# Flipping P and x in 64-row halves, with one PSUM tile of two banks for both

## The chip, the cores and the metric

One core of a Trainium2 chip runs the program. The metric is the device time of one execution in microseconds (us). Engines are named as the profile names them: PE (TensorE matmul), PEld (its weight loads), DVE (VectorE), ACT (ScalarE), POOL (GpSimd), SP (SyncE, which issues DMAs).

## The reference

Attention over 8 batches, 8 heads, 576 tokens of 64 elements, with a causal window of 128 and a linear bias by head, and then a soft mixture of 8 experts with 4 slots each, on all 4608 tokens of 512 elements. Shapes and eps aside it is

```python
scores = q @ k.T / 8 ; scores = where(0 <= rel < 128, scores - slope * abs(rel), -1e9)
attn = softmax(scores) @ v                     # per batch and head
x = attn.transpose(0, 2, 1, 3).reshape(4608, 512)
logits = x @ phi                               # 4608 x 32 slots
d = softmax(logits, axis=0); slot_input = d.T @ x
h = relu(slot_input[e] @ w1[e]); slot_out = h @ w2[e]      # per expert e
out = softmax(logits, axis=1) @ slot_out
```

## The kernel before

A group is (b, t, g): batch b, a tile t of 128 tokens (t = 4 is the tail of 64), and half g of the heads, four heads to a group; the tail takes all eight. There are 72 groups. Scores and softmax have tokens on the partitions, so that row sums are free. The product with V needs P with keys on the partitions, and the logits and the dispatch sums need x both ways. So PE turns 128x128 pieces over by a matmul with the identity as moving operand: `flip` does it for the four pieces of P of a group (from `p4`, L351), `x_flip` for the four pieces of a token tile of x (L408). Each writes one PSUM bank: P goes to tile `pt`, x to tile `xq`. ACT copies them out, P in `split` (L358, to `pa`; on POOL two affine selects then part it into the strips before and on the diagonal), x in `x_keep` (L417, to `xn`).

PSUM has 8 banks of 512 fp32 elements per partition. Before, four banks are the tags xp, mi, pt, xq of `ps_1`, one tile each, and two score tiles `s4` have two banks each. At the end of the loop some flips go `to=` a bank that is free.

All engines run in the order that the code writes (`tc.manual_schedule`). Iteration i of the loop issues: `softmax_front` of group i on DVE (merge of the two key strips, row maximum, bias `nb`, inverse, and `normalise`, L306, of group i-1); `flip` and `split` of group i-3; copies due now ("act"); `values` of group i-4 (L387, P times V); the scores of group i+1 (L247/L254, for t = 0 L235/L240); `expo` (L341: four exponentials on ACT, which wait for `nb`, L292); and what is due late ("pe": `x_flip`, `logits`, `slot_flip` L465, `token_flip`, `slot_sum`, `slot_tail` L516; "dve": `token_max` L451, `slot_add` L522). `slot_sum` multiplies the dispatch weights of a batch with its x into `ap`, and `slot_add` adds that to `acc` with a rescaling, as an online softmax does. Odd batches b < 7 take the tail of two batches along: `slot_tail` adds it, and there alone `x_keep` stands in the "pe" list, which on ACT is behind the exponentials:

```python
            if tail:
                do("pe", i + 2, x_flip, b, 4)
                do("pe", i + 4, x_keep, b, 4)
                do("pe", i + 5, slot_tail, b)
                do("dve", i + 5, slot_add, b)
```

After the loop (here called the end of the attention) the last four groups ga, gb, gc, gd run by a list of their own: `flip(gb)`, `values(gb, ..., bank("xq"))`, `lane_rows`, `slot_sum(last)`, `join` (L601, adds up the lanes), `join_keep` (ACT, L604), `last_sum` (L651, copied by DVE, L654), `slot_inputs` (L660, which needs POOL's `comb`, L606). Then come the experts (`hidden` L931, `expert_out` L967) and the final combination (L991, L993).

Of the kernel before, what the change touches and what calls it, by code (L numbers as in the profile page):

```python
# [10 lines left out]
F32 = mybir.dt.float32  # L11
# [10 lines left out]
DM = H * D  # L22
E, SPE, F = 8, 4, 1024
NS = E * SPE
P = 128
# [43 lines left out]
def tile_attn_softmoe(  # L69
# [88 lines left out]
    front = ctx.enter_context(ExitStack())  # L158
    ps_s = front.enter_context(tc.tile_pool(name="ps_s", bufs=1, space=PSUM))
    s4s = [ps_s.tile([P, 4, 2 * P], F32, name=f"s4_{i}") for i in range(2)]  # L160
    free = [s4[:, 2 * h:2 * h + 2].rearrange("p u w -> p (u w)") for s4 in s4s for h in range(2)]
# [64 lines left out]
    def scores(i):  # L226
# [3 lines left out]
        if i == 0:  # L230
            parts = [ps_1.tile([P, 2, 2 * P], F32, tag=tag, name="s4_0") for tag in ("pt", "xp")]
        qt = qs[i % 3].rearrange("p (j w) -> p j w", w=width(t))
# [113 lines left out]
    def flip(key, us=ALL, to=None):  # L346
        s = st[key]
        if "pt" not in s or to is not None:
            s["pt"] = ps_1.tile([P, 4, P], F32, tag="pt", name="pt") if to is None else to
        for u in range(4)[us]:  # L350
            nc.tensor.transpose(s["pt"][:, u], s["p4"][:, u], ident)  # L351

    def split(key, us=ALL):
        s, t = st[key], key[1]
        i = number[key] % 2 if number[key] < n - 1 else 2
        m = len(range(4)[us])
        pa, pp = pas[i], pps[i % 2]
        nc.scalar.copy(pa[:, us], s["pt"][:, us])  # L358
        if 0 < t < 4:
            nc.gpsimd.affine_select(  # L360
                pp[:, us], pa[:, us], [[0, m], [-1, P]], ALU.is_gt, 0.0, base=0, channel_multiplier=1)
            nc.gpsimd.affine_select(  # L362
                pa[:, us], pa[:, us], [[0, m], [1, P]], ALU.is_ge, 0.0, base=0, channel_multiplier=-1)
        elif t == 4:
            nc.gpsimd.affine_select(
                pp[:, us], pa[:, us], [[0, m], [0, 2], [-1, TAIL]], ALU.is_gt, 0.0, base=0, channel_multiplier=1)
            nc.gpsimd.affine_select(
                pa[0:TAIL, us], pa[0:TAIL, us], [[0, m], [0, 2], [1, TAIL]], ALU.is_ge, 0.0,
                base=0, channel_multiplier=-1)
        s.update(pd=pa, pp=pp)  # L370
# [34 lines left out]
    def x_flip(b, t, to=None):  # L405
        xq = ps_1.tile([P, DM], F32, tag="xq", name="xq") if to is None else to
        for j in range(NPAIR):
            nc.tensor.transpose(xq[:, P * j:P * j + P], x_of(b, t)[:, j], ident)  # L408
        st["xq", b, t] = xq
# [6 lines left out]
    def x_keep(b, t, copy=nc.scalar.copy):  # L416
        copy(xn_of(b, t), st.pop(("xq", b, t)))  # L417

# [86 lines left out]
    def slot_sum(b):  # L505
        dn = st["d", b]
        ap = ps_1.tile([P, DM], F32, tag="mi" if b < last else "pt", name="ap")
        for c in range(lanes(b)):
            nc.tensor.matmul(
                ap[NS * c:NS * c + NS], lhsT=dn[:, NS * c:NS * c + NS], rhs=xns[c],  # L510
                start=True, stop=(c < 3 or not with_tail(b)),
            )
        st["a", b] = ap
# [85 lines left out]
    def join():  # L599
        st["join"] = ps_1.tile([P, 512], F32, tag="pt", name="join")  # L600
        nc.tensor.matmul(st["join"][fin], lhsT=comb, rhs=acc, start=True, stop=True)  # L601
# [45 lines left out]
    def last_sum(h):  # L647
        ap = ps_1.tile([P, DM // 2], F32, tag=("xq", "xp")[h], name="ap")
        cols = slice(DM // 2 * h, DM // 2 * (h + 1))
        for c in range(3):  # L650
            nc.tensor.matmul(  # L651
                ap[NS * c:NS * c + NS], lhsT=st["dnf"][:, NS * c:NS * c + NS],
                rhs=xn_of(last, FINAL[c])[:, cols], start=True, stop=True)
        (nc.scalar.copy if h else nc.vector.tensor_copy)(sums[0:3 * NS, cols], ap[0:3 * NS])  # L654
# [122 lines left out]
    with tc.manual_schedule(engines=ORDERED):  # L777
# [34 lines left out]
        def bank(tag):  # L812
            return ps_1.tile([P, NPAIR, P], F32, tag=tag, name="bank")

# [4 lines left out]
        token_copy(last)  # L819
        flip(gb)  # L820
        split(gb, LO)
# [15 lines left out]
        values(gb, range(0, 2), bank("xq"))  # L837
        flip(gd, LO)
        split(gd, LO)
# [30 lines left out]
        load_weight()  # L870
        x_flip(last, 4)
        x_flip(last, 0, free[1])
# [34 lines left out]
    front.close()  # L907
    ps_o = ctx.enter_context(tc.tile_pool(name="ps_o", bufs=4, space=PSUM))

    def load_weights(k):  # L910
# [11 lines left out]
    def hidden(nb, kk):  # L922
        if kk == 0:
            hp[nb] = ps_1.tile([P, 512], F32, tag=("xp", "pt")[nb], name="hp")
        for g in range(2):
# [20 lines left out]
    def hidden_flip(nb):  # L946
        hq = ps_1.tile([P, 512], F32, tag="xq", name="hq")
        for i in range(4):
# [9 lines left out]
    def expert_out(m, f, g):  # L958
        w = MW[m]
        if m not in ops:  # L960
            ops[m] = ps_1.tile([P, w], F32, tag=("xp", "pt")[m % 2], name="op")
        fu = UW // w
# [17 lines left out]
    def slot_stack(j):  # L980
        ot = ps_1.tile([P, P], F32, tag=("xq", "mi")[j % 2], name="ot")
        for i in range(2):
# [139 lines left out]
```

## Time and profile before

| | |
|---|---|
| median of 3 runs | 296.63 us (296.41 to 296.80) |
| span of the profiled execution | 294.4 us; the median of the runs is 2.2 us longer (no time of its own is given for this execution) |
| PE busy | 94% of the span |
| DVE busy | 82% |
| ACT busy | 71% |
| POOL busy | 32% |
| flips of P, PE (L351) | 282 matmuls, 45.9 us |
| flips of x, PE (L408) | 136 matmuls in tile xq, 22.1 us |

Busy times of PE overlap between successive matmuls, so the time a group of them takes is read from the distance of their starts. In rows of the timeline the columns are the start in us from the span's start, the duration of the group, engine, line, operation, output and inputs, shapes, the number of instructions, and in brackets the idle time before with what ended it. The body of the loop lies between about 17 and 217 us.

### The profile page before, as it was taken

The page shows a single profiled execution, that of the slowest core. Times are in us where ns is not written, and L with a number is a line of the kernel's source. Part 1 is how long each engine was busy: PE and PEld are TensorE (multiplying, and loading weights), DVE is VectorE, ACT ScalarE, POOL GpSimd, SP SyncE. Part 2 cuts the span into 40 slices and gives each one's busy share as a digit, 9 for nine tenths or more (in the row PEclk, how much of TensorE's full clock was granted, in tenths as well). Part 3 has the DMA queues.
Part 4 walks back from the last instruction along what each step waited for, and adds up shares of the span by engine and source line. Part 5 has one row for each costly group of instructions (what it writes and reads, how often), then busy time and mean ns, then how long its engine had stood idle before and what let it go on. Part 6 is the DMA issues. An engine that isn't in the chain of part 4 may idle for free. (4 is left out here: it accounts for less than half of the span.)

```text
span 294.4 us, 13061 instructions
## 1 busy us (share of the span) xinstructions
PE 275.9 (94%) x5131; PEld 195.7 (66%) x5131; DVE 240.3 (82%) x745; ACT 208.2 (71%) x814; POOL 93.0 (32%) x207
## 2 busy tenths in 40 slices
PE   8598999999999999999999999999999999999980
PEld 4366777777677777776776777667766743587650
DVE  3889999999989999998999999979996454655450
ACT  2778898987988988987898978978886421044450
POOL 2033525542444354244415442445452011000000
PEclk9689999999999999999999999999999999999997
DMA  6635368878676887868588967776456599998997
GB/s 192 217 112 144 110 194 251 277 218 288 203 265 209 268 284 235 260 213 273 180 281 262 292 217 248 248 222 222 141 164 234 160 314 355 411 400 327 345 365 264
DMA packets 36754, 72.59 MB, mean 247 GB/s; under 512 B 4402, under 2 KB 15316, under 8 KB 36692
## 3 DMA queue, kind: packets, MB, share of 16 engines
q1 hardware_dynamic: 35972, 71.24, 72.8%
q8 instruction: 41, 0.67, 0.9%
q10 hardware_dynamic: 720, 0.51, 0.6%
q14 instruction: 21, 0.17, 0.2%
HBM read 62.29 MB, written 9.44 MB: 244 GB/s over the span
## 5 line engine op out<-in xcount | busy, mean ns | idle before, releaser
L341 ACT ACTIVATE area<-s,nb 128x128 f32<-128x128 f32 x288 | 102.3, 375 | 19.8 <-DVE nb L292 17.5
L306 DVE TENSOR_SCALAR area<-area,rs 128x128 f32<-128x128 f32 x286 | 79.5, 339 | 0.7 <-DVE nb L292 0.3
L387 PE MATMUL xp<-area 128*64 128x128 f32 (+1 forms) x1104 | 75.4, 272 | 1.1 <-POOL rs L297 0.4
L387 PEld LDWEIGHTS xp<-area 128*64 128x64 f32 x1104 | 56.5, 137 | 15.9 <-issue 9.3
L341 ACT ACTIVATION_READ_ACCUMULATOR area<-s,nb 128x1 f32 x288 | 61.3, 213 | 0.0
L289 DVE TENSOR_REDUCE s<-s 128x4 f32<-128x512 f32 x71 | 49.5, 698 | 2.2
L358 ACT COPY area<-pt 128x512 f32<-128x512 f32 (+1 forms) x72 | 42.3, 590 | 11.6 <-PE pt L351 11.3
L351 PE MATMUL pt<-unit_r,area 128*128 128x128 f32 x282 | 45.9, 285 | 2.7 <-ACT area L306 2.2
L297 POOL TENSOR_SCALAR rs<-sm 128x4 f32<-128x4 f32 x70 | 13.8, 197 | 99.0 <-ACT area L341 98.2
L351 PEld LDWEIGHTS pt<-unit_r,area 128*128 128x128 f32 x282 | 32.0, 143 | 17.2 <-PE s L254 5.0
L254 PE MATMUL s<-kq 64*32 64x160 f32 x1792 | 42.4, 303 | 0.1
L360 POOL TENSOR_SCALAR_AFFINE_SELECT area<-area 128x512 f32<-128x512 f32 x48 | 31.4, 655 | 26.7 <-ACT area L358 25.6
L269 DVE COPY_PREDICATED s<-cst,s 128x512 f32<-128x512 int32 x48 | 32.9, 686 | 1.3 <-PE s L254 1.3
L362 POOL TENSOR_SCALAR_AFFINE_SELECT area<-area 128x512 f32<-128x512 f32 x48 | 31.5, 657 | 3.3
L254 PEld LDWEIGHTS s<-kq 64*32 64x32 f32 x1792 | 29.9, 108 | 1.0 <-issue 0.4
L408 PE MATMUL xq<-unit_r,area 128*128 128x128 f32 x136 | 22.1, 285 | 0.8 <-ACT area L417 0.7
L403 ACT COPY area<-xp 128x512 f32<-128x512 f32 (+1 forms) x37 | 20.7, 559 | 2.9 <-PE xp L387 2.3
L247 PE MATMUL s<-ramp,ones 64*32 64x320 bf16 x448 | 18.9, 313 | 2.7 <-ACT area L341 2.2
L417 ACT COPY area<-xq 128x512 f32<-128x512 f32 x34 | 20.7, 608 | 0.2 <-PE xq L408 0.2
L408 PEld LDWEIGHTS xq<-unit_r,area 128*128 128x128 f32 x136 | 14.5, 141 | 7.4 <-issue 4.1
L993 ACT COPY ob<-po 128x512 f32<-128x512 f32 x19 | 10.4, 591 | 11.4 <-PE po L991 10.7
L993 DVE COPY ob<-po 128x512 f32<-128x512 f32 x17 | 11.2, 687 | 6.6 <-PE po L991 5.8
(169 smaller groups left out, 328.4 us busy)
## 6 DMA issues: line engine op xcount, KB each, us to landing
w<-w SPq DMA_DIRECT2D x53, 512.0 KB, 5.2
out<-ob SPq DMA_DIRECT2D x36, 256.0 KB, 3.9
kq<-q_t SPq DMA_DIRECT2D x69, 128.0 KB, 3.2
kq<-k_t SPq DMA_DIRECT2D x32, 256.0 KB, 3.8
area<-v_n SPq DMA_DIRECT2D x31, 256.0 KB, 4.2
area<-w SPq DMA_DIRECT2D x8, 512.0 KB, 4.8
area<-v_n SPq DMA_DIRECT2D x12, 128.0 KB, 3.1
kq<-w SPq DMA_DIRECT2D x3, 512.0 KB, 6.3
```

Source lines behind the costliest of these rows:

```text
L254: nc.tensor.matmul(s4[32 * c:32 * c + 32, 2 * par + jj, 32 * r:32 * r + WIN], lhsT=qt[rows, 2 * h + jj if t == 4 else jj, 32 * r:32 * r + 32],
L269: nc.vector.copy_predicated(s4[:, :, P:2 * P], bc(mask_u, 1, 4), s4[:, :, 0:P])
L289: nc.vector.tensor_reduce(st[key]["mx"][:, us], merged(key, us), axis=AX.X, op=ALU.max, negate=True)
L306: mul(p4[:, u], p4[:, u], st[key]["rs"][:, u:u + 1])
L341: nc.scalar.activation(s["p4"][:, u], merged(key, u), AF.Exp, bias=s["nb"][:, u:u + 1], scale=SCALE, accum_out=s["sm"][:, u:u + 1],)
L351: nc.tensor.transpose(s["pt"][:, u], s["p4"][:, u], ident)
L358: nc.scalar.copy(pa[:, us], s["pt"][:, us])
L360: nc.gpsimd.affine_select(pp[:, us], pa[:, us], [[0, m], [-1, P]], ALU.is_gt, 0.0, base=0, channel_multiplier=1)
L362: nc.gpsimd.affine_select(pa[:, us], pa[:, us], [[0, m], [1, P]], ALU.is_ge, 0.0, base=0, channel_multiplier=-1)
L387: nc.tensor.matmul(xp[D * par:D * par + D, j, 0:w], lhsT=v_slot[b, t - 1 + ph][0:rows, D * h:D * h + D], rhs=src[:, 2 * par + i] if t < 4 ...
L408: nc.tensor.transpose(xq[:, P * j:P * j + P], x_of(b, t)[:, j], ident)
L993: copy_by[by](ob, po)
```

## The change

One tile `pq` of two banks takes the place of the tags pt and xq. The columns 0 to 255 of both banks belong to P, 256 to 511 to x. A piece is no longer one transpose of 128 rows but two of 64 rows, which stand on the upper and the lower half of PE's rows; row half r writes bank r. `split` and `x_keep` read their halves from both banks. 69 of the 72 flips of P and 33 of x are made so. The flips with `to=` at the end of the attention stay whole, and use single banks of `pq` (or of `s4`); the tiles for `join`, `last_sum(0)`, the last `slot_sum` and others of the end, which had been tiles of the tags pt and xq, are now parts of `pq` too. The experts' tiles get a pool of their own (`ps_2`) after `pq` is freed. Waits are set by the tile: what writes any part of `pq` waits for the copies that still read it.

```diff
+    pq = ps_s.tile([P, 2, 4 * P], F32, name="pq")
+    pq_p, pq_x = pq[:, :, 0:2 * P], pq[:, :, 2 * P:4 * P]
...
     def flip(key, us=ALL, to=None):
         s = st[key]
-        if "pt" not in s or to is not None:
-            s["pt"] = ps_1.tile([P, 4, P], F32, tag="pt", name="pt") if to is None else to
+        if to is not None:
+            s["pt"] = to.rearrange("p u (r w) -> p u r w", r=2)
+            for u in range(4)[us]:
+                nc.tensor.transpose(to[:, u], s["p4"][:, u], ident)
+            return
+        s["pt"] = pq_p.rearrange("p r (u w) -> p u r w", u=4)
         for u in range(4)[us]:
-            nc.tensor.transpose(s["pt"][:, u], s["p4"][:, u], ident)
+            for r, rows in enumerate(half):
+                nc.tensor.transpose(s["pt"][:, u, r], s["p4"][rows, u], ident[rows, rows])
...
-        nc.scalar.copy(pa[:, us], s["pt"][:, us])
+        nc.scalar.copy(pa[:, us].rearrange("p u (r w) -> p u r w", r=2), s["pt"][:, us])
...
     def x_flip(b, t, to=None):
-        xq = ps_1.tile([P, DM], F32, tag="xq", name="xq") if to is None else to
+        x = x_of(b, t)
+        if to is not None:
+            for j in range(NPAIR):
+                nc.tensor.transpose(to[:, P * j:P * j + P], x[:, j], ident)
+            st["xq", b, t] = to.rearrange("p (j r w) -> p j r w", j=NPAIR, r=2)
+            return
+        xq = pq_x.rearrange("p r (j w) -> p j r w", j=NPAIR)
         for j in range(NPAIR):
-            nc.tensor.transpose(xq[:, P * j:P * j + P], x_of(b, t)[:, j], ident)
+            for r, rows in enumerate(half):
+                nc.tensor.transpose(xq[:, j, r], x[rows, j], ident[rows, rows])
         st["xq", b, t] = xq
...
-        copy(xn_of(b, t), st.pop(("xq", b, t)))
+        copy(xn_of(b, t).rearrange("p (j r w) -> p j r w", j=NPAIR, r=2), st.pop(("xq", b, t)))
...
-        ap = ps_1.tile([P, DM], F32, tag="mi" if b < last else "pt", name="ap")
+        ap = ps_1.tile([P, DM], F32, tag="mi", name="ap") if b < last else pq[:, 0]
...
-        st["join"] = ps_1.tile([P, 512], F32, tag="pt", name="join")
+        st["join"] = pq[:, 0]
...
-        ap = ps_1.tile([P, DM // 2], F32, tag=("xq", "xp")[h], name="ap")
+        ap = ps_1.tile([P, DM // 2], F32, tag="xp", name="ap") if h else pq[:, 1, 0:DM // 2]
...
-            return ps_1.tile([P, NPAIR, P], F32, tag=tag, name="bank")
+            return pq[:, ("pt", "xq").index(tag)].rearrange("p (u w) -> p u w", u=4)
...
-        flip(gb)
+        flip(gb, to=bank("pt"))
...
-        flip(gd, LO)
+        flip(gd, LO, bank("pt"))
...
-        x_flip(last, 4)
+        x_flip(last, 4, pq[:, 1])
```

No instruction changes its place on an engine; the flips become longer lists, and waits change. Line numbers of the changed kernel are larger by 3 to 18: `flip` is L359 in halves and L354 whole, `x_flip` L423 and L417, `split` L366, `x_keep` L432, `slot_tail` L531, `slot_add` L537.

The first place is on PE, at the tail of an odd batch. Before, between the last of `slot_sum` and `slot_tail`:

```order
L509 MATMUL ap<-area,dn 32x512 x3
L351 MATMUL pt<-unit_r,area 128x128 [waits PE_49]
L351 MATMUL pt<-unit_r,area 128x128 x3
L387 MATMUL xp<-area 64x128 [waits Activation_49,Pool_49]
L387 MATMUL xp<-area 64x128
```

and now:

```order
L524 MATMUL ap<-area,dn 32x512 x3
L359 MATMUL pq<-unit_r,area 128x64 [waits Activation_49]
L359 MATMUL pq<-unit_r,area 128x64 x7
L395 MATMUL xp<-area 64x128 [waits PE_49,Pool_49]
L395 MATMUL xp<-area 64x128
```

The flip of P has 8 matmuls of half the width, and waits for ACT's count now. The copy that it waits for is the x_keep of the tail tile, which on ACT stands here, in the changed kernel, behind the four exponentials and ahead of this flip's own copy:

```order
L344 ACTIVATE area,sm<-s_1_84,nb 128x128 [waits DVE_49,Pool_49]
L344 ACTIVATE area,sm<-s_1_84,nb 128x128 x3
L432 COPY area<-pq 128x512 [waits PE_49]
L366 COPY area<-pq 128x512 [waits PE_49,Activation_49,Pool_49]
L552 ACTIVATE ln<-ln 128x160
```

Before, the same two copies stood in the same order there, out of two tiles (xq and pt). A little further on the same PE list follow the scores of t = 0 (L243, 64 rows and 128 columns), the flip of x and `slot_tail`; now:

```order
L243 MATMUL s_1_84<-kq 128x128 [waits DMAHW4_49]
L243 MATMUL s_1_84<-kq 128x128 x3
L423 MATMUL pq<-unit_r,area 128x64 [waits Activation_49]
L423 MATMUL pq<-unit_r,area 128x64 x7
L531 MATMUL ap<-area,dn 32x512
```

Here the order is as it was; the flip of x has the array shape of the scores ahead of it.

The second place is on PE at the end of the attention, around `flip(gb)`. Before:

```order
L426 MATMUL lp<-area,phi 32x128 [waits DVE_49]
L426 MATMUL lp<-area,phi 32x128 x7
L351 MATMUL pt<-unit_r,area 128x128 [waits PE_49]
L351 MATMUL pt<-unit_r,area 128x128 x3
L465 MATMUL dp<-unit_r,lg 128x64 [waits Activation_49]
```

and now:

```order
L441 MATMUL lp<-area,phi 32x128 [waits DVE_49]
L441 MATMUL lp<-area,phi 32x128 x7
L354 MATMUL pq<-unit_r,area 128x128 [waits Activation_49]
L354 MATMUL pq<-unit_r,area 128x128 x3
L480 MATMUL dp<-unit_r,lg 128x64 [waits Activation_49]
```

The flip is whole in both; its wait for PE's own count has become one for ACT, the copy of the x tile flipped just before.

The third place is on DVE, where the last `slot_add` stands. Before:

```order
L596 TENSOR_SCALAR comb<-cst,rows 128x32 [waits PE_49]
L597 TENSOR_TENSOR lg<-lg,rows 1x128 [waits Activation_49]
L522 SCALAR_TENSOR_TENSOR acc<-acc,al,ap 64x512 [waits PE_49]
L633 COPY dn<-dp 128x96 [waits DVE_49,PE_49]
L580 TENSOR_REDUCE lg<-lg 1x32 [waits DVE_49]
L654 COPY area<-ap 96x256 [waits PE_49]
```

and now:

```order
L611 TENSOR_SCALAR comb<-cst,rows 128x32 [waits PE_49]
L612 TENSOR_TENSOR lg<-lg,rows 1x128 [waits Activation_49]
L537 SCALAR_TENSOR_TENSOR acc<-acc,al,pq 64x512 [waits Activation_49]
L648 COPY dn<-dp 128x96 [waits DVE_49,PE_49]
L595 TENSOR_REDUCE lg<-lg 1x32 [waits DVE_49]
L669 COPY area<-pq 96x256 [waits PE_49,Activation_49]
```

`slot_add` and the copy of `last_sum` now wait for ACT's copies as well.

More of the change, by code (lines that the diff above doesn't have):

```diff
@@ L230, in scores @@
         if i == 0:
-            parts = [ps_1.tile([P, 2, 2 * P], F32, tag=tag, name="s4_0") for tag in ("pt", "xp")]
+            parts = [ps_1.tile([P, 2, 2 * P], F32, tag="xp", name="s4_0"), pq[:, 0].rearrange("p (u w) -> p u w", u=2)]
+            parts = parts[::-1]
         qt = qs[i % 3].rearrange("p (j w) -> p j w", w=width(t))
@@ L908, in tile_attn_softmoe @@
     ps_o = ctx.enter_context(tc.tile_pool(name="ps_o", bufs=4, space=PSUM))
+    ps_2 = ctx.enter_context(tc.tile_pool(name="ps_2", bufs=1, space=PSUM))
+    bank_of = {"xp": ps_1, "mi": ps_1, "pt": ps_2, "xq": ps_2}
     def load_weights(k):
@@ L923, in hidden @@
         if kk == 0:
-            hp[nb] = ps_1.tile([P, 512], F32, tag=("xp", "pt")[nb], name="hp")
+            tag = ("xp", "pt")[nb]
+            hp[nb] = bank_of[tag].tile([P, 512], F32, tag=tag, name="hp")
         for g in range(2):
@@ L946, in hidden_flip @@
     def hidden_flip(nb):
-        hq = ps_1.tile([P, 512], F32, tag="xq", name="hq")
+        hq = ps_2.tile([P, 512], F32, tag="xq", name="hq")
         for i in range(4):
@@ L960, in expert_out @@
         if m not in ops:
-            ops[m] = ps_1.tile([P, w], F32, tag=("xp", "pt")[m % 2], name="op")
+            tag = ("xp", "pt")[m % 2]
+            ops[m] = bank_of[tag].tile([P, w], F32, tag=tag, name="op")
         fu = UW // w
@@ L980, in slot_stack @@
     def slot_stack(j):
-        ot = ps_1.tile([P, P], F32, tag=("xq", "mi")[j % 2], name="ot")
+        tag = ("xq", "mi")[j % 2]
+        ot = bank_of[tag].tile([P, P], F32, tag=tag, name="ot")
         for i in range(2):
```

## The prediction

> **What bounds the kernel now.** I read the page's busy table first, then a table of busy time over a window, and then DVE's waits.
>
> ```profile
> PE 275.9 (94%) x5131; PEld 195.7 (66%) x5131; DVE 240.3 (82%) x745; ACT 208.2 (71%) x814; POOL 93.0 (32%) x207
> ```
>
> PE looks like the bound, with 94% of the 294.4 us span. But the span holds stages with different limits: the attention loop to about 217 us, its end to 239, and then the experts. So I take a window inside the attention loop: two periods of two batches, 63.38 to 172.94. Columns: length; busy time of PE, PEld, DVE, ACT, POOL; granted clock, DMA share, GB/s.
>
> ```profile
> 63.38:172.94 109.56, 108.48 (x2192) 79.73 (x2185) 104.22 (x333) 94.58 (x390) 44.13 (x97) 1.00 0.77 247
> ```
>
> PE is 1.1 us short of full and DVE 5.3. Which of the two sets the pace is told by who waits. DVE's waits on others from 60 to 215 us (columns: total, times, longest) are these two alone:
>
> ```profile
> DVE acc L522 <- PE ap L516: 4.1, 3, 1.5
> DVE fine L451 <- ACT lg L446: 1.6, 3, 0.5
> ```
>
> Six waits, 5.7 us in 155. Between them DVE runs without a stop, so a faster PE gains nothing there: a microsecond off PE counts only where it shortens one of these six. PE is late for DVE at two places per odd batch: slot_tail (L516), whose sum slot_add (L522) takes, and the token copy (L446) behind PE's logits.
>
> **What a flip costs, and in halves.** These rows show a flip of four pieces in the loop, then weight loads by shape (mean ns after the busy time), then three small transposes.
>
> ```profile
> 86.24 0.66 PE L408 MATMUL xq<-unit_r,area 128*128 128x128 f32 x4
> 86.73 0.60 PE L351 MATMUL pt<-unit_r,area 128*128 128x128 f32 x4
> 87.26 0.99 PE L387 MATMUL xp<-area 128*64 128x128 f32 x14
> ```
> ```profile
> L351 PEld LDWEIGHTS pt<-unit_r,area 128*128 128x128 f32 x282 | 32.0, 143 | 17.2 <-PE s L254 5.0 <-ACT area L341 4.8 <-issue 2.9
> L240 PEld LDWEIGHTS s<-kq 64*128 64x128 f32 x128 | 9.4, 207 | 0.2
> L983 PEld LDWEIGHTS ot<-so,ostk 128*128 128x128 f32 x8 | 1.4, 188 | 0.6 <-DVE so L977 0.2 <-DVE so L978 0.2
> L676 PEld LDWEIGHTS dp<-unit_r,lg 32*128 32x128 f32 x3 | 0.3, 136 | 0.9 <-issue 0.9
> ```
> ```profile
> 245.70 0.26 PEld L676 LDWEIGHTS dp<-unit_r,lg 32*128 32x128 f32 x3 [0.86 <-issue]
> ```
>
> A flip takes 86.73−86.24 = 0.49 to 87.26−86.73 = 0.53 us of PE's time, about 0.12 a piece. Fewer rows do not shorten a load of 128 columns (136 ns with 32 rows, 143 with 128). But small loads can follow faster: three span 0.26 us, (0.26−0.136)/2 = 62 ns apart. And loads into the two row halves of the array (L240) take 207 ns each beside 188 for a lone one (L983), so a pair seems to cost little more than one. In halves a piece is two loads of 64 rows and two streams of 64 columns. Bounds: nothing saved (a pair costs what one piece did) and 0.19 us a flip (a pair at about 75 ns against 0.12). I take 0.12 us a flip, a piece at some 90 ns: the loads remain and only the streams are halved. 102 flips (69 of P, 33 of x) in halves make some 12 us of PE work, of which DVE's pace hides all but what reaches the six waits.
>
> By the Trainium skill ("TensorE: Matmul & The Clock Gate", LDWEIGHTS) a load takes its columns divided by 1.2, 107 ns for 128 columns, whatever the rows. Loads 62 ns apart at L676 disagree with it as a pace. By it a flip would stay at some 0.43 us and save at most 0.1, which is rival 2.
>
> **The new waits.** P and x now share two banks in one tile, so each flip of P must let ACT's copy of x (x_keep) end, and each flip of x ACT's copy of P (split). At most places the copy ends before PE gets there, mostly by 0.3 us or more. Not so at the tail of an odd batch, b = 1, 3, 5:
>
> ```profile
> 79.13 0.16 DVE L292 TENSOR_SCALAR nb<-s 128x4 f32<-128x4 f32 x1
> 80.13 0.66 PE L351 MATMUL pt<-unit_r,area 128*128 128x128 f32 x4
> 80.42 0.37 ACT L341 ACTIVATE area<-s,nb 128x128 f32<-128x128 f32 x1
> 80.77 0.60 ACT L417 COPY area<-xq 128x512 f32<-128x512 f32 x1
> 82.40 0.66 PE L408 MATMUL xq<-unit_r,area 128*128 128x128 f32 x4
> 82.99 1.04 PE L516 MATMUL ap<-area,dn 128*32 128x512 f32 x2
> 84.07 0.75 DVE L522 SCALAR_TENSOR_TENSOR acc<-acc,al,ap 128x512 f32<-128x512 f32 x1 [1.34 <-PE ap L516]
> ...
> 189.69 0.66 PE L351 MATMUL pt<-unit_r,area 128*128 128x128 f32 x4
> ...
> 190.34 0.59 ACT L417 COPY area<-xq 128x512 f32<-128x512 f32 x1
> ```
>
> The x_keep of the tail tile stands on ACT behind the four exponentials, which DVE's nb (79.13) released, and ends at 81.37. PE's flip of P began at 80.13. With the wait it can begin at 81.42: +1.29 us (190.34+0.59 against 189.69: 1.24 and the same handover). Behind it on PE stand values, the next scores, the x flip and slot_tail, without a gap, and for slot_tail DVE has been waiting 1.34 us already. So the delay goes through, less what PE saves on the way: two flips at 0.12, and one change of array shape, since the scores of t=0 (64x128) now stand ahead of a flip of that same shape (82.99−82.40 = 0.59 against 0.49–0.53: 0.09). Net 1.29−0.24−0.09 = +0.96 us, three times: **+2.9**. Bounds each: +0.67 (flips 0.19 faster, and another 0.15 regained as DVE's work moves) to +1.29.
>
> The Trainium skill ("PSUM — Partial Sum Buffer", PSUM bank collisions raise a hardware error) says that PSUM is to be guarded by bank and quadrant and not by address. By it the wait is there although P and x lie in other columns, and the sum is this +0.96; were columns enough, the same place would gain, as in rival 1. No run here shows a collision.
>
> **The token copy.** DVE waits 0.52 us at
>
> ```profile
> 72.83 0.42 DVE L451 TENSOR_REDUCE fine<-lg 128x1 f32<-128x256 f32 x1 [0.52 <-ACT lg L446]
> ```
>
> at the end of a chain that a flip of P, ACT's split and two copies make. If two of the flips ahead of it shorten that chain by 0.12 each, that is −0.25, **−0.75** for three (bounds −1.56, the whole wait, and +0.5).
>
> **The start.** DVE waits for the first scores behind a flip:
>
> ```profile
> 13.06 1.12 PE L351 MATMUL pt<-unit_r,area 128*128 128x128 f32 x4
> 14.11 1.12 PE L387 MATMUL xp<-area 128*64 128x128 f32 x8
> ...
> 16.83 0.70 DVE L269 COPY_PREDICATED s<-cst,s 128x512 f32<-128x512 int32 x1 [1.09 <-PE s L254]
> ```
>
> A flip costs 14.11−13.06 = 1.05 us there, double of what it costs later, so the gain doubles to some 0.24: **−0.2** (0 to −0.4).
>
> **The end of the attention.** From 218 us each engine waits for another. The flips and sums there move into the shared tile.
>
> ```profile
> 219.67 0.60 ACT L417 COPY area<-xq 128x512 f32<-128x512 f32 x1
> 220.33 0.66 PE L408 MATMUL xq<-unit_r,area 128*128 128x128 f32 x4 [0.65 <-ACT area L417]
> ...
> 221.91 0.66 PE L351 MATMUL pt<-unit_r,area 128*128 128x128 f32 x4
> 222.40 0.60 ACT L417 COPY area<-xq 128x512 f32<-128x512 f32 x1
> 223.19 0.27 PE L465 MATMUL dp<-unit_r,lg 64*128 64x64 f32 x1 [0.62 <-ACT lg L444]
> ...
> 226.29 0.98 PE L387 MATMUL bank<-area 128*64 128x64 f32 x16
> 226.40 0.37 ACT L358 COPY area<-pt 128x256 f32<-128x256 f32 x1
> ```
>
> A handover from ACT to PE takes 0.06 us (220.33 − 219.67 − 0.60). The flip at 221.91 must now wait for the x_keep that ends at 223.00, and begins at 223.06; the transposed logits (L465) then begin at 223.06+0.58 = 223.64 instead of 223.19: +0.45. The values at 226.29 write a bank of the tile that ACT's split reads until 226.77; they wait for it, 0.54 more. Sum **+1.0** (bounds 0.5 to 1.1).
>
> ```profile
> 234.09 0.74 DVE L522 SCALAR_TENSOR_TENSOR acc<-acc,al,ap 64x512 f32<-64x512 f32 x1
> 234.67 0.58 ACT L417 COPY area<-xq 128x512 f32<-128x512 f32 x1 [0.24 <-PE xq L408]
> 235.30 1.04 PE L601 MATMUL join<-acc,comb 128*32 128x512 f32 x2
> 235.81 1.06 PE L651 MATMUL ap<-area,dn 128*32 128x256 f32 x12
> 236.38 0.58 ACT L604 COPY area<-join 32x512 f32<-32x512 f32 x1 [0.64 <-PE join L601]
> 236.52 0.42 DVE L654 COPY area<-ap 96x256 f32<-96x256 f32 x1 [0.59 <-PE ap L651]
> 237.59 0.63 PE L660 MATMUL s<-comb,area 128*128 128x32 f32 x4 [0.57 <-POOL comb L606]
> 238.61 7.17 PE L931 MATMUL hp<-w,acc 128*32 128x512 f32 x64
> ```
>
> slot_add (234.09) now waits for ACT's x_keep, which ends at 235.25, and the join comes 0.8 late, at 236.10. (Times here are those before, without the +1.0.) The first half of last_sum (235.81) lies in the tile too and must wait for ACT's copy of the join, now 0.8 later (237.18 to 237.76), so it begins at 237.82. DVE's copy of it followed 0.71 behind (236.52) and lasts 0.42: it ends at 238.95, and slot_inputs (237.59, held by POOL till now) begins at about 239.00: **+1.4** (bounds 0.8, the first wait alone, and 1.5). Behind it PE is full to the end (238.61, 7.17 us in one block), so all of it stays.
>
> **What costs nothing.** ACT issues as many instructions as before, and its copies read two banks in runs of 64: no row shows such a read; the nearest are the plain copies at 0.60 us, and I take the same, 0 to 0.05 more, which stands beside idle time on ACT except at the end. The final experts keep their instructions; DMA queues are untouched.
>
> **Sum.** +2.9 −0.75 −0.2 +1.0 +1.4 = +4.35 us on the profiled span of 294.4, so 298.7; the median of the runs, 296.63, is 2.2 above that span, which I keep: **300.9 us**.
>
> **Rivals.**
> 1. Faster: the flips of P meet no unfinished x_keep. PE is ahead of its copies only by DVE's pace; if DVE's nb (79.13) came 1.3 us earlier against PE, x_keep would be done at 80.1 and PE would arrive at slot_tail five flips and one change of shape sooner, 0.7 us off each of the three waits of 1.34. Then −2.1−0.75−0.2 = −3.05, if the end gave nothing back: 293.6. Against it: DVE has no wait between 72.83 and here that could give it 1.3 us. The point from which it decides: x_keep ending by 80.07. Chance 0.08.
> 2. Halves save nothing, since loads of a pair follow each other: three times 1.29−0.09, no gain at tokens and start, +2.4 at the end: +6.0, 302.6. For it the load row L676 (as long with 32 rows as with 128); against it L240. Chance 0.2.
> 3. The end hides its waits, as its chain has slack that I overrate as tight: +2.9−0.95 = +1.95, 298.6. For it: POOL, not DVE, held slot_inputs. Chance 0.15.
> 4. Losses and gains meet near nothing: 0.05.
>
> **The numbers.** My forecast, at 0.52, spreads by its terms' bounds: low +2.0−1.56−0.4+1.3 = +1.35, 298.0; high +3.9+0.5+0+2.6 = +7.0, 303.6, which takes in rivals 2 and 3. Range 297.9 to 303.5, with some 0.15 outside. Under 0.2% (0.6 us) a measurement of this kernel tells no change. Faster 0.08 (rival 1), same 0.05 (rival 4), slower 0.87.
>
> **What would show it.** Right: each 8-piece flip about 0.37–0.40 us to the next instruction; three flips of P waiting some 1.2 us for ACT's copy of x, and DVE's waits for slot_tail 2.2–2.4 instead of 1.34–1.47; token waits under 0.3; PE's flip at the end waiting for x_keep, and DVE's last slot_add for ACT. Body from 17 to 217 us longer by 2, the stretch from there to hidden by 2.4. Wrong: if x_keep is no longer behind the exponentials in time, if the flips take 0.5 us still (rival 2), or if copies of two banks take visibly over 0.6 us, which would move every x_keep and split.

## The result, and the profile after

The changed kernel takes 306.17 us (median of 4 runs, 303.70 to 307.51) against 296.72 of the kernel before: a ratio of 1.031 (95% interval 1.027 to 1.036), 9.4 us slower. The forecast was 300.9, at most 303.5: the sign is right, the size is not. The profiled execution, with a span of 305.8 us, is the longest of the four (307.51). The runs differ by more than those of the kernel before, and a reason for that shows below.

First the busy table and the granted clock in 40 slices (10 tenths of full speed are shown as 9):

```profile
PE 266.3 (87%) x5539; PEld 187.2 (61%) x5539; DVE 239.4 (78%) x745; ACT 208.6 (68%) x814; POOL 93.2 (30%) x207
PEclk9799999999999999997999999899997999999997
```

PE has 9.6 us less work and yet the span is 11.4 longer. The clock is under full speed in slices in which it was full before. What each flip cost shows in the starts of neighbours:

```profile
205.06 0.46 PE L423 MATMUL pq<-unit_r,area 64*128 64x64 f32 x8
205.36 0.41 PE L359 MATMUL pq<-unit_r,area 64*128 64x64 f32 x8
205.70 1.17 PE L395 MATMUL xp<-area 128*64 128x128 f32 x16
```

0.30 and 0.34 us, against 0.49 and 0.53: the halves do stand side by side, and a flip saves 0.19 us. The copies out of two banks cost nothing more; by shape, before and then after (the second number behind the bar is the mean in ns):

```profile
L358 ACT COPY area<-pt 128x512 f32<-128x512 f32 x69 | 41.3, 599 | 11.6 <-PE pt L351 11.3
L417 ACT COPY area<-xq 128x512 f32<-128x512 f32 x34 | 20.7, 608 | 0.2 <-PE xq L408 0.2
```
```profile
L366 ACT COPY area<-pq 128x512 f32<-128x512 f32 x69 | 41.5, 601 | 17.0 <-PE pq L359 16.2 <-POOL rs L300 0.7
L432 ACT COPY area<-pq 128x512 f32<-128x512 f32 x34 | 20.7, 609 | 0.3 <-PE pq L417 0.3
```

Where the time went is read from the start of the same instruction in both traces; DVE sets the pace, so its instructions are the milestones. The distance is the start after less the start before:

| milestone | before | after | distance |
|---|---|---|---|
| DVE, a merge of batch 0 | 41.55 | 40.39 | −1.16 |
| slot_add of batch 0 | 53.05 | 54.01 | +0.96 |
| token_max of batch 1 | 72.83 | 73.61 | +0.78 |
| slot_add of batch 1 | 84.07 | 85.61 | +1.54 |
| slot_add of batch 3 | 138.89 | 142.53 | +3.64 |
| slot_add of batch 5 | 193.78 | 200.15 | +6.37 |
| token_max of batch 6 | 211.71 | 218.58 | +6.87 |
| experts begin (hidden, PE) | 238.61 | 249.55 | +10.94 |

The three waits of PE at the odd tails are there, and DVE's waits for slot_tail behind them. Two of the three are far longer than the third (PE's rows, then DVE's):

```profile
82.21 0.46 PE L359 MATMUL pq<-unit_r,area 64*128 64x64 f32 x8 [1.36 <-ACT area L432]
...
137.58 0.56 PE L359 MATMUL pq<-unit_r,area 64*128 64x64 f32 x8 [1.82 <-ACT area L432]
138.07 1.97 PE L395 MATMUL xp<-area 128*64 128x128 f32 x16
...
194.97 0.46 PE L359 MATMUL pq<-unit_r,area 64*128 64x64 f32 x8 [1.82 <-ACT area L432]
```
```profile
85.61 0.75 DVE L537 SCALAR_TENSOR_TENSOR acc<-acc,al,ap 128x512 f32<-128x512 f32 x1 [2.46 <-PE ap L531]
...
142.53 0.75 DVE L537 SCALAR_TENSOR_TENSOR acc<-acc,al,ap 128x512 f32<-128x512 f32 x1 [4.00 <-PE ap L531]
...
200.15 0.75 DVE L537 SCALAR_TENSOR_TENSOR acc<-acc,al,ap 128x512 f32<-128x512 f32 x1 [4.24 <-PE ap L531]
```

The values behind the second wait take 1.97 us instead of the 1.09 of the same group before. Busy time by windows tells why (length; PE, PEld, DVE, ACT, POOL busy; then the granted clock):

```profile
79.77:83.19 3.42, 2.06 (x34) 1.07 (x28) 3.29 (x15) 2.38 (x10) 0.55 (x2) 1.00 0.77 240
134.39:137.80 3.41, 1.59 (x38) 0.43 (x24) 3.28 (x13) 2.33 (x10) 1.15 (x3) 1.00 0.94 316
137.80:141.21 3.41, 3.41 (x38) 2.96 (x36) 0.73 (x4) 2.22 (x10) 1.47 (x3) 0.50 0.41 133
226.55:229.96 3.41, 1.46 (x24) 1.12 (x24) 2.31 (x8) 2.67 (x13) 1.46 (x2) 1.00 0.98 356
229.96:233.37 3.41, 3.27 (x22) 2.49 (x22) 2.23 (x11) 0.87 (x4) 1.47 (x4) 0.50 0.69 249
```

From 137.80 to 141.21 PE ran at half clock, and again at 195.82 and 229.96, for 3.41 us each time. In the 3.41 us ahead PE had been busy 1.59, 1.59 and 1.46 us. Ahead of the first tail's end it was busy 2.06, and the clock stayed. A half-clock window on the path costs about 1.6 us: by the distance of DVE's slot_add against that of the instruction ahead of it, the second tail added 2.29 us, the third 2.39, the first 0.75. Two runs that come below keep the same three waits with halves, the repeat of this kernel and the version with the old end; over the nine tails of the three traces, the four with a half-clock window behind the wait added 2.29 to 2.42 us, the five others 0.75 to 0.91. PE waited 1.80 to 1.82 us at eight of the nine (1.36 at the first tail here), so the length of the wait does not decide alone. The Trainium skill ("TensorE: Matmul & The Clock Gate", What's actually happening) describes such a gate, which halves the clock after a window of 3413 ns with too little activity and whose windows run free of the program. The trace agrees: each stretch lasts 3.41 us, and the three begin 58.02 and 34.14 us apart, 17 and 10 times 3.413.

A further loss: in batch 0 PE stood for 0.96 us with nothing in the profile that it waited for ("issue"), and DVE waited for slot_sum where it had not before:

```profile
52.48 0.47 PE L257 MATMUL s<-kq 64*32 64x160 f32 x7 [0.96 <-issue]
```
```profile
54.01 0.69 DVE L539 COPY acc<-ap 128x512 f32<-128x512 f32 x1 [1.55 <-PE ap L524]
```

And at the end of the attention stand the waits that the prediction named (PE's rows, then DVE's):

```profile
227.37 0.46 PE L423 MATMUL pq<-unit_r,area 64*128 64x64 f32 x8 [1.14 <-ACT area L432]
...
230.10 1.11 PE L354 MATMUL pq<-unit_r,area 128*128 128x128 f32 x4 [1.27 <-ACT area L432]
...
235.74 0.98 PE L395 MATMUL pq<-area 128*64 128x64 f32 x16 [0.46 <-ACT area L366]
...
247.24 0.63 PE L666 MATMUL pq<-area,dn 128*32 128x256 f32 x6 [0.67 <-ACT area L619]
...
249.55 2.85 PE L949 MATMUL hp<-w,acc 128*32 128x512 f32 x24
```
```profile
244.74 0.74 DVE L537 SCALAR_TENSOR_TENSOR acc<-acc,al,pq 64x512 f32<-64x512 f32 x1 [1.32 <-ACT area L432]
```

### The profile page after: what moved, and what is told of

Same layout as the page of the kernel before. It is cut to its first block, busy times and chain, and to the rows that moved or that the text cites. A ratio compares the mean times of both kernels' runs of the same rounds, so it can differ in the third digit from the quotient of the medians.

```text
span 305.8 us, 13833 instructions
## 1 busy us (share of the span) xinstructions
PE 266.3 (87%) x5539; PEld 187.2 (61%) x5539; DVE 239.4 (78%) x745; ACT 208.6 (68%) x814; POOL 93.2 (30%) x207
## 4 chain that ended last, share of the span: by engine, by line
DVE 45%; PE 35%; ACT 8%; issue 5%; POOL 2%; DMA 1%; DVEq 0%; ACTq 0%; POOLq 0%
DVE area L309 15%; DVE s L292 11%; DVE s L272 6%; ACT area L344 6%; PE op L986 5%; PE xp L395 5%; PE hp L949 5%; PE po L1011 3%; PE s L257 3%; DVE s L270 3%; PE pq L359 1%; DVE acc L537 1%; PE s L250 1%; DMA area<-v_n 1%; DVE rs L304 1%
## 5 line engine op out<-in xcount | busy, mean ns | idle before, releaser
L395 PE MATMUL xp<-area 128*64 128x128 f32 (+1 forms) x1104 | 79.4, 278 | 4.1 <-DMA area<-v_n 1.6
L309 DVE TENSOR_SCALAR area<-area,rs 128x128 f32<-128x128 f32 x286 | 78.1, 334 | 0.8 <-DVE nb L295 0.3
L395 PEld LDWEIGHTS xp<-area 128*64 128x64 f32 x1104 | 58.2, 139 | 14.3 <-POOL area L370 2.9
L344 ACT ACTIVATION_READ_ACCUMULATOR area<-s,nb 128x1 f32 x286 | 60.5, 212 | 0.0
L366 ACT COPY area<-pq 128x512 f32<-128x512 f32 (+1 forms) x72 | 42.5, 592 | 18.2 <-PE pq L359 16.2
L257 PE MATMUL s<-kq 64*32 64x160 f32 x1792 | 43.5, 303 | 1.2 <-issue 1.2
L359 PE MATMUL pq<-unit_r,area 64*128 64x64 f32 x552 | 32.1, 233 | 10.4 <-ACT area L432 5.7
L359 PEld LDWEIGHTS pq<-unit_r,area 64*128 64x128 f32 x552 | 23.6, 139 | 26.6 <-ACT area L432 12.2
L432 ACT COPY area<-pq 128x512 f32<-128x512 f32 x34 | 20.7, 609 | 0.3 <-PE pq L417 0.3
L250 PEld LDWEIGHTS <-ones 64*32 64x32 bf16 x448 | 8.3, 89 | 16.6 <-issue 12.4
L1013 ACT COPY ob<-po 128x512 f32<-128x512 f32 x19 | 10.4, 591 | 11.4 <-PE po L1011 9.7
L423 PE MATMUL pq<-unit_r,area 64*128 64x64 f32 x264 | 15.4, 236 | 1.6 <-ACT area L432 1.1
```

Source lines behind the costliest of these rows:

```text
L250: nc.tensor.matmul(s4[32 * c:32 * c + 32, 2 * par:2 * par + 2, 32 * r:32 * r + WIN], lhsT=ones[rows, 0:32], rhs=ramp[rows, h], start=True, ...
L257: nc.tensor.matmul(s4[32 * c:32 * c + 32, 2 * par + jj, 32 * r:32 * r + WIN], lhsT=qt[rows, 2 * h + jj if t == 4 else jj, 32 * r:32 * r + 32],
L309: mul(p4[:, u], p4[:, u], st[key]["rs"][:, u:u + 1])
L344: nc.scalar.activation(s["p4"][:, u], merged(key, u), AF.Exp, bias=s["nb"][:, u:u + 1], scale=SCALE, accum_out=s["sm"][:, u:u + 1],)
L359: nc.tensor.transpose(s["pt"][:, u, r], s["p4"][rows, u], ident[rows, rows])
L366: nc.scalar.copy(pa[:, us].rearrange("p u (r w) -> p u r w", r=2), s["pt"][:, us])
```

## The experiments

Two theories stood after this. Theory A: the three waits at the tails and those at the end, each with the half clock that may follow, are nearly all of the loss. Theory B: the halves themselves cost, by more PE instructions and copies out of two banks, and the waits only show a PE that would be late anyway. Each version was timed beside the kernel before. Where a saving is given "by the ratios", it is the difference of the ratios to the kernel before, times 296.4 us.

**The early copy.** The tail's x_keep moves ahead of the exponentials, by one iteration, into a buffer of its own.

```diff
+    x_tail = wpool.tile([P, UW], F32, tag="w", name="x_tail")[:, 0:DM]
...
-        return xns[lane(b, t)] if t < 4 else xns[3]
+        return xns[lane(b, t)] if t < 4 else x_tail
...
-                do("pe", i + 4, x_keep, b, 4)
+                do("act", i + 3, x_keep, b, 4)
```

> The changed kernel, with the copy x_keep of the tail tile moved ahead of the exponentials (one iteration earlier, into a buffer of its own), so that no flip of P stands behind it. Theory A (the three waits of PE of 1.36 to 1.82 us at the tails of odd batches, and the clock of 0.5 that follows two of them, are most of the loss): no such wait, clock 1.00 around them, DVE's waits for slot_tail about 1.1 us each instead of 2.46, 4.00 and 4.24, so 7.4 us less in the profiled execution: 298 to 300 us. Theory B (the halves themselves cost: more PE instructions, stalls of PE's issue, copies out of two banks, and PE would be late without these waits as well): at most 2 us less, 304 to 306.

Measured: 299.52 us, ratio 1.008 (1.005 to 1.012), 6.7 us less than the change. Of DVE's waits for slot_tail, which had been 10.7 us in all, this is left (columns: total, times, longest):

```profile
DVE acc L538 <- PE ap L532: 0.3, 1, 0.3
```

That is less than the 1.1 us each that were expected. At each tail the distance of slot_add falls by 1.6 to 1.7 us against the instruction just ahead of it, and by 1.0 to 1.2 us against the slot_add of the batch before; the rest only makes up for DVE being later just ahead, as it is by 0.9 us in the kernels with the early copy and whole flips too. What the prediction hoped for from faster flips is there as soon as nothing waits. So three waits, with what follows them, were nearly three quarters of the loss, and theory B falls as it was put: it allowed 2 us at most. The trace still shows two windows of half clock (155.0 and 206.2).

**The waits without the halves.** Whole flips, P in one bank of the shared tile and x in the other.

```diff
     def flip(key, us=ALL, to=None):
         s = st[key]
+        if to is None:
+            to = pq[:, 0].rearrange("p (u w) -> p u w", u=4)
...
     def x_flip(b, t, to=None):
         x = x_of(b, t)
+        if to is None:
+            to = pq[:, 1]
```

> The changed kernel with whole flips again, P in one bank of the shared tile and x in the other: as many PE instructions and the same copies as before the change, only the waits of the shared tile remain. Theory A: PE's waits at the three tails about 1.25 us, DVE's for slot_tail about 2.6 each (+3.7 in all) if the clock stays at 1.00, and the end of the attention 2.4 to 3.7 longer: 302.5 to 304; each place where the clock falls adds 1.6, to 307 at most. Theory B (the halves cost): 297 to 299, the waits alone hardly matter.

Measured: 302.48 us, ratio 1.023 (1.017 to 1.029).

```profile
81.15 0.65 PE L356 MATMUL pq<-unit_r,area 128*128 128x128 f32 x4 [1.23 <-ACT area L436]
```
```profile
DVE acc L541 <- PE ap L535: 9.1, 3, 3.1
```

Each tail adds 1.29 us to DVE's distance (84.07 against 85.09, 1.02 later, from −0.26 just before; the other two alike), exactly the wait as the prediction priced it. P and x lie in different banks here and the wait is there all the same, so it comes with the shared tile and not with a shared bank. No window of half clock follows in the body: PE comes later to the wait, since its flips are slower, and waits 1.23 and not 1.82 us. So with the waits in place, the faster flips seem to have made the kernel slower: 1.031 with halves, 1.023 without. The intervals overlap a little (from 1.027 and up to 1.029).

**A shorter wait.** x_keep of the tail goes between the second and the third exponential.

```diff
-                do("pe", i + 4, x_keep, b, 4)
+                do("half", i + 4, x_keep, b, 4)
...
+            if ("half", i) in todo:
+                run("pe", i)
+                expo(new, LO)
+                run("half", i)
+                expo(new, HI)
```

> The changed kernel with the x_keep of the tail tile put between the second and the third of the four exponentials instead of behind the fourth: PE's wait there becomes shorter by two exponentials, 0.7 us, and is not taken away. If a long wait costs more than itself because the clock falls behind it (theory A): waits of 0.6 to 1.1 us, clock 1.00, DVE's waits for slot_tail 1.8 to 2.0 each, some 5 us less in all: 300 to 302. If the price goes with the length of the wait alone: 3 x 0.7 = 2.1 less, 304.

Measured: 300.79 us, ratio 1.018 (1.012 to 1.023), 4.0 us less than the change by the ratios. PE waits 1.12 us, the clock in the windows there stays full, and DVE's waits for slot_tail are far shorter:

```profile
134.36 0.46 PE L359 MATMUL pq<-unit_r,area 64*128 64x64 f32 x8 [1.12 <-ACT area L432]
```
```profile
133.28:136.69 3.41, 2.33 (x43) 2.03 (x43) 2.84 (x10) 3.41 (x17) 1.22 (x3) 1.00 0.84 272
```
```profile
DVE acc L537 <- PE ap L531: 1.8, 3, 0.8
DVE rs L304 <- POOL rs L300: 1.4, 3, 0.5
```

That is more than the 2.1 us that go with the wait's length, as theory A has it, but by the two intervals the saving is anything between 2 and 6 us, so the time alone does not decide. The trace does: PE waits 1.11 to 1.12 us at all three tails, and no window of half clock stands in the body. The waits of DVE, 0.5 to 0.8 each, fell well below the 1.8 to 2.0 expected of each: the later exponentials hold DVE up too (three waits for the inverse sums from POOL, 1.4 us in all), so a part of the loss only moved.

**PE busy instead of waiting.** This is the test of the clock by itself: twelve transposes of the identity stand ahead of the waiting flip, into the bank that `values` overwrites next. They are useless work.

```diff
+    def busy(i):
+        b, t, g = groups[i - LAG]
+        if (b, t) not in st:
+            st[b, t] = ps_1.tile([P, NPAIR, P], F32, tag="xp", name="xp")
+        for k in range(12):
+            nc.tensor.transpose(st[b, t][:, 2 * g + k % 2], ident, ident)
...
                 do("pe", i + 4, x_keep, b, 4)
+                do("fill", i + 5, busy, i + 5)
...
+            run("fill", i)
             if i + near >= FLAG and i != SKIP:
                 flip(groups[i + near - FLAG])
```

> The changed kernel with twelve extra whole transposes on PE ahead of the flip of P that waits at the three tails; they turn the identity over into the bank that values overwrites next, at 0.11 us each about 1.3 us. They make no work shorter and no copy earlier: PE is busy instead of waiting. If PE's idle time is what lowers the clock there (theory A): no clock of 0.5 behind these places, DVE's waits for slot_tail about 2.5 us each instead of up to 4.2, some 3 us less than the changed kernel: a ratio of 1.020 to 1.024. If the low clock has another cause, or the lateness comes from the waits alone: the same as the changed kernel, 1.028 to 1.034, or more by what the extra work delays.

Measured: 303.06 us, ratio 1.026 (1.020 to 1.033); the changed kernel on the same chip, run again beside it, 306.95 us, 1.036 (1.029 to 1.043):

> The changed kernel unaltered, on the same chip as the two others. Expected 1.031 again, with runs apart by 2 to 4 us, since the windows of low clock fall differently in each run.

The profiled execution with the extra work has no window of half clock at any tail, and none anywhere before its last microseconds:

```profile
81.51 0.46 PE L359 MATMUL pq<-unit_r,area 64*128 64x64 f32 x8 [0.34 <-ACT area L439]
```
```profile
140.15 0.75 DVE L544 SCALAR_TENSOR_TENSOR acc<-acc,al,ap 128x512 f32<-128x512 f32 x1 [2.47 <-PE ap L538]
...
195.88 0.75 DVE L544 SCALAR_TENSOR_TENSOR acc<-acc,al,ap 128x512 f32<-128x512 f32 x1 [2.95 <-PE ap L538]
```
```profile
PEclk9999999999999999999999999999999999999996
```

The wait for x_keep ends as late as before, and DVE's waits come down from 4.00 and 4.24 to 2.47 and 2.95. Giving PE work to do while it waits saved 3.9 us by the medians, 2.8 by the ratios. The ratio of 1.026 lies between the two forecasts (1.020 to 1.024, and 1.028 or more), and its interval overlaps that of the repeat, so the time alone leaves it open. In the repeated run of the changed kernel a half-clock window follows the second tail (137.98) and not the third: it is a matter of how the free-running windows fall, which spreads its runs (304.71 to 308.35 here). At the begin of the experts the trace with the extra work is 3.8 us ahead of that of the repeat; 1.6 of it come at the second tail, and 1.4 at the end of the attention, where the repeat has a half-clock window and this run has none. No half clock at three tails fits theory A, but five of the nine tails without extra work kept their clock as well, so this one trace does not prove it by itself.

**The old end.** From group 66 on, whole flips, and P and x in banks and tiles of their own.

```diff
+CUT = 66
...
+            if i == CUT:
+                quick.close()
+                own.append(ctx.enter_context(tc.tile_pool(name="ps_2", bufs=1, space=PSUM, side="right")))
...
     def x_flip(b, t, to=None):
         x = x_of(b, t)
+        if to is None and own:
+            to = whole("xq")
```

`quick.close()` frees `pq`; `flip`, `join`, `last_sum` and the last `slot_sum` get tiles of their own likewise.

> The changed kernel with the shared tile given up from group 66 on: there whole flips, P and x in banks and tiles of their own as before the change. What the shared tile costs at the end of the attention: DVE's distance to the kernel before grows from 6.9 us (at 218 us) to 10.6 (at 250) in the profiled execution, so 3.7 us less: 302.5 (theory A: two waits of 1.3 and 1.1 us, a clock of 0.83 between 230 and 240, and the join behind ACT). By the prediction's sum it would be 2.4 less: 303.8. If the end is late for other reasons (weights, the start of DMAs): 0 to 1 less.

Measured: 302.42 us, ratio 1.021 (1.014 to 1.029), 1.0% or 2.9 us less than the change by the ratios. That is between the prediction's 2.4 and the 3.7 of the trace, in which a half-clock window takes a part; the interval is too wide to tell the two apart. In its trace the end of the attention costs nothing: the distance is +5.31 at the slot_add of batch 6 and +5.32 at the experts.

**Both together.** The early copy and the old end: halves in the body, with none of the new waits that cost.

> The changed kernel without either of its new waits: the early x_keep of the tail tile, and from group 66 on whole flips in tiles of their own. What is left is the halves in the body. Theory A: the two savings add (1.0084 for the early copy, 0.0098 for the end): 295 to 297, a ratio of about 0.999; PE is 0.19 us a flip faster, which DVE's pace hides, and DVE's waits for slot_tail are under 0.3. If the halves bring what the prediction gave them (0.7 at each slot_tail, tokens, start) and the clock costs nothing: 293.5. If they cost something by themselves (issue stalls, clock): 297 to 299.

Measured: 293.60 us, ratio 0.990 (0.987 to 0.993), 2.8 us faster than the kernel before. That is more than the sum of the two gave: theory A's 0.999 was too timid, and 293.5, the forecast for halves that bring their gain, was met. DVE's waits for slot_tail, and the begin of slot_inputs and of the experts (238.61 before):

```profile
DVE acc L552 <- PE ap L546: 0.6, 2, 0.3
```
```profile
237.57 0.63 PE L690 MATMUL s<-comb,area 128*128 128x32 f32 x4 [0.57 <-POOL comb L636]
238.03 0.61 PE L690 MATMUL pt<-comb,area 128*128 128x32 f32 x4
238.58 7.16 PE L967 MATMUL hp<-w,acc 128*32 128x512 f32 x64
```

In the profiled execution, the slowest but one of its six, the tails gain 0.7, 1.1 and 1.0 us against the slot_add of the batch before. Batch 4 spends 2.7 us of it again, on one stall and the half clock that followed it, and batch 6 another 0.95:

```profile
155.16 0.27 PE L372 MATMUL pq<-unit_r,area 64*128 64x64 f32 x1 [1.89 <-issue]
```
```profile
152.30:155.74 3.44, 1.55 (x40) 0.98 (x17) 3.34 (x11) 1.90 (x10) 1.21 (x3) 1.00 0.84 269
155.74:159.15 3.41, 3.41 (x61) 2.18 (x59) 1.62 (x7) 2.34 (x12) 1.58 (x3) 0.50 0.27 100
```

Four of the six runs took 292.92 to 293.77 us; none of these was traced, so where their gain lies is not seen.

**The same two without halves.** Two kernels with whole flips and the early copy, the first with the shared tile to the end, the second with the old end.

```diff
-        s["pt"] = pq_p.rearrange("p r (u w) -> p u r w", u=4)
+        whole_p = pq[:, 0].rearrange("p (u w) -> p u w", u=4)
+        s["pt"] = whole_p.rearrange("p u (r w) -> p u r w", r=2)
         for u in range(4)[us]:
-            for r, rows in enumerate(half):
-                nc.tensor.transpose(s["pt"][:, u, r], s["p4"][rows, u], ident[rows, rows])
+            nc.tensor.transpose(whole_p[:, u], s["p4"][:, u], ident)
```

> The kernel with whole flips in the shared tile, with the early x_keep: neither halves nor the three waits, only the waits at the end. Theory A: the kernel before plus the end alone, 2.4 to 3.7 more: 298.6 to 300; against the early copy with halves (1.0084) it tells what the halves are worth when nothing waits. If the shared tile costs in the body at other places too: over 301.

> As the version with the early x_keep and the old end (0.990), but with whole flips in the body, P in one bank of the shared tile and x in the other. It tells whether the 1% comes from the halves or from the early copy. Theory A (from the halves: three waits for slot_tail that vanish, 1.4 to 1.7 us each in the trace, less some PE stalls): 1.000, within 0.4%. If from the early copy and the end alone: 0.990 to 0.993.

Measured: 298.21 us, 1.008 (1.005 to 1.011), and 295.48 us, 0.999 (0.996 to 1.001). The second is the kernel before to within its interval: neither the early copy nor the old end brings anything of itself, and the 0.9% between 0.999 and 0.990 are, in this pair, the halves. With the shared end the same comparison gives nothing: 1.008 with halves (the early copy) and 1.008 without. In the trace of the early copy the tails gain 3.3 us, but batches 4 and 6 lose 2.1 and 2.3, each with a half-clock window, against 0.0 and 1.1 with whole flips. So the halves are worth 0.9% in one pair and nothing in the other, and why is not settled. The step between the two versions with whole flips, 0.9% or 2.8 us, is the price of the shared tile at the end. From 1.023 to 1.008, 4.4 us, is that of the three waits without halves: 3 x 1.29 = 3.9, and half a microsecond more.

## Why the prediction was wrong

- **What bounds the kernel: right.** DVE paces the body; 9.6 us less PE work showed only at the places where DVE waits for PE.
- **The cost of a flip: the bound, not the value.** 0.12 us saved was forecast between 0 and 0.19; it was 0.19. A pair of 64-row pieces takes about 80 ns (0.30 to 0.34 us for four). The Trainium skill ("TensorE: Matmul & The Clock Gate", LDWEIGHTS) gives a load's columns divided by 1.2, an estimate of 107 ns for 128 columns. These traces do not bear that out as a pace. Rival 2 is refuted.
- **The three tails: the place and the wait right, the size wrong.** +0.96 each was forecast. Where the clock stayed it was +0.75 (first tail), near the sum with the true saving (1.29−2×0.19−0.09 = 0.82). The other two cost 2.29 and 2.39. The step that failed is "the delay goes through, less what PE saves on the way": it took the work behind the wait to run at the speed of the trace before. There the clock halved for 3.41 us, some 1.6 us each, **+3.2 us** that no term held. The trace before shows the same 0.5 from 10.3 to 17.1 us; the prediction used the doubled flip there and not its cause. And the sign of the saving seems to have turned: a PE that is ahead waits longer (1.80 to 1.82 us at eight of nine tails, against 1.23 with whole flips), and only behind waits of that length did the clock fall at a tail.
- **Token copies: right.** −0.21 each instead of −0.25, the waits now 0.31.
- **The start: −1.16 instead of −0.2**, since its half-clock stretch was one window of 3.41 us (11.5 to 14.9) and not two (10.3 to 17.1). Other runs of kernels with halves begin between −1.5 and −0.2, so this is no gain of the change to count on.
- **The end: the waits right, the sum too small.** +2.4 was forecast; DVE and PE went from +6.87 to +10.94, 4.1 us. One half-clock window (229.96 to 233.37) is in it. From the slot_add of batch 6 to the experts, the shared end cost 2.9 to 3.0 us in the three traces that have no such window there (the early copy with halves and with whole flips, and PE kept busy), and 3.9 to 4.4 in the four that have one. So the sum was some 0.5 us too small and the clock added 1.0 to 1.5. Without halves the shared end cost 2.8 us by the ratios.
- **Not foreseen:** the stalls of PE's issue, a term that the prediction did not have (the last section tells where they stand). Three of them (0.38, 0.49 and 0.96 us) stand in batch 0, which lost 2.1 us here; batch 4 lost 0.5, with one of 0.28. And the V tiles of batch 7 came late (0.5 us of DVE's distance at 215.8): PE waited 1.58 us for them here, and 1.05 to 2.23 at the same place in the traces of all the other versions, whole or halved, against 0.36 in the one trace before. Why is open.
- **Rival 1 was right in its price.** It gave 293.6 for flips of P that meet no unfinished x_keep and an end that gives nothing back, and the version with both edits measured 293.60. That the two agree so closely is luck: in its trace the tails gain 0.7 to 1.1 us each, and the start and batches 4 and 6 move by 0.8 to 2.7. The prediction was right that the condition does not hold in this kernel.

In the profiled execution the sum is −1.2 (start) +2.1 (batch 0) +5.4 (tails) −0.6 (tokens) +0.5 (batch 4) +0.5 (V) +4.1 (end), with +0.1 elsewhere, 10.9 at the experts. The medians lie 9.4 us apart and the two profiled executions 11.4; the one after was the slowest of its four.

## What to carry to other kernels

Sharing a PSUM tile between two streams ties each stream's writer to the other's reader; ask for every such pair where the reader stands in its queue, and move that one instruction before paying for the shared tile. Here one copy moved ahead of four exponentials, and the shared tile given up where only latency counts, turned 1.031 into 0.990. A wait on PE can have a second price, the clock of what follows it: count PE's busy time around the wait, not only the wait. And more, shorter instructions may have a price of their own, where PE runs through its list faster than the list comes in.

## What the runs showed of the hardware

- Idle time of PE well short of a whole window lowered the clock. Behind waits of 1.80 to 1.82 us at a tail the clock fell to 0.50 for 3.41 us at four of eight tails; behind waits of 1.36 us and less, at none of ten (the first tail after, whole flips, the shorter wait, PE busy). It fell behind two stalls of PE's issue too, of 1.32 and 1.89 us. The Trainium skill ("TensorE: Matmul & The Clock Gate", HAM oscillation) gives as the abstract rule that PE should have no idle gaps over some 3.4 us. In these traces shorter ones sufficed. Busy shares of 0.43 to 0.47 of the window ahead were followed by half clock in the changed kernel, 0.60 was not; but in other traces of this study one of 0.47 was not followed by it, and three of 0.86 were, so the threshold is not settled by busy time alone.
- PE's stalls with nothing shown to wait for (0.2 to 1.9 us) appeared in the traces of five of the six kernels with halves (not in the one with the shorter wait), and in the four with whole flips once, 0.3 us. The traces tell where they stand. If all entries of PE are counted, those of its sequencer too, every one of these 15 stalls ends at the 194th or 195th of a block of 256, and 1.2 to 1.6 us behind the end of a DMA packet of 16,384 bytes of the kind "instruction". Such packets make up queue 8 (packets, MB, share; before, then after):

```profile
q8 instruction: 41, 0.67, 0.9%
q8 instruction: 44, 0.72, 0.9%
```

There is one for some 255 of PE's entries (10441 before, 11211 after). So PE stood there for the next piece of its own program, as far as these records tell; a flip in halves runs through 16 loads and matmuls in 0.30 to 0.34 us, a whole one through 8 in 0.49 to 0.53. Why the piece came late at some blocks and not at others stays open. A version of the kernel before with two transposes of 64 columns for each piece, meant to show the larger number of instructions without the shared tile, gave no measurement.
